# A PSUM bank by name for every tile, and a new order for the loading phase of a fused cross-attention and gated feed-forward kernel

## The chip, the cores and the metric

The kernel runs on one core of a Trainium2 chip. The metric is the device time of one execution in microseconds (us). Several executions are timed and their median is the kernel's time; one more execution is recorded by the hardware profiler, and all rows of a profile come from that one.

## The reference, cut to what matters

```python
B, H, S, Ns, D = 8, 8, 512, 32, 64            # x (B, H, S, D), state (B, H, Ns, D)
a  = softmax(x @ state.T / sqrt(D))           # per batch and head, 512 x 32
xread = a @ state                             # 512 x 64
a2 = softmax(state @ x.T / sqrt(D))           # 32 x 512
sread = a2 @ x                                # 32 x 64
attn = concatenate([xread, sread], axis=2)    # 544 rows for each batch and head
X = attn.transpose(0, 2, 1, 3).reshape(8 * 544, 512)
out = (sigmoid(X @ w_gate) * (X @ w_val)) @ w_out   # w_gate, w_val 512 x 1536, w_out 1536 x 512
```

## The kernel before, in words

All matrix operands are bf16, sums are fp32. For a batch `b` the kernel never forms `xread`. It multiplies the state with the weights first (`sw_visit`, `sw_wide`, `sw_six`: `SW` = state x `w_gate` and state x `w_val`, 128 rows for a group of heads) and then multiplies that with the transposed attention `aT` (`gv_mm`, `gv_half`, L345 and L357): the result is the gate and the value product of 128 hidden features for the 512 rows of the batch. ScalarE takes the tanh of one half (`gv_th`, L366), VectorE makes the gated product from it and the other half (`gv_glu`, L371). The product with `w_out` is done plainly for batch 0 (`out_mm`, L384) and in seven products of half the size, in Strassen's manner, from then on (`w_mm`, L427, with the sums of `t_sum` and `s_sum`). The `sread` rows of all batches are handled together at the end as a ninth batch (L360, L446, L463).

The steps for one batch's attention: `xT_mm` transposes x on TensorE (batches 0 and 1) or `at_xT_dma` does so by DMA (later ones); `S_mm` or, for batch 0 by quarters, `Sq_mm` makes the scores; `S_exp`/`Sq_exp` the exponential on ScalarE; `n_sum`/`nq_sum` and `n_mul`/`nq_mul` the softmax's sums and the scaled `ab`; `aT_mm` with `aT_cp`, or `aT_dma`, the transpose `aT`; `at_Eb` casts the exponentials and `rd_mm` with `rd_fin` makes the `sread` rows.

The schedule is by hand: every engine runs its instructions in the order in which the program issues them. PSUM has eight banks, each of which holds one tile. In the kernel before they belong to four pools: `GV` (two banks), `SWP` (four), `OU` and `AT` (one each); a pool with several banks gives each new tile one of its own, and the matmul that writes it waits for the last reader of the tile that had it.

The program has two parts. The first, a flat list of calls from `pre = wp.tile(...)` to `rd_fin(2)`, loads and casts everything, does all of batches 0 and 1 but the end of batch 1's output product, and prepares batch 2. The loads stand on three queues: SP has `load_xp(0, ...)` (four parts of x(0)), later `load_x(3)`, the DMA transposes and the stores; POOL has `load_xh(1, ...)`, ten weight loads `load_w(w, lo, n)` (w 0 is the gate, 1 the value; `lo` the first hidden column), three `load_sb`, three `load_wo` and `load_x(2)`, mixed with its own casts and products; ScalarE's has `load_s(0)`. `warm(n, bank)` issues n matmuls on a zero tile (L496), which compute nothing that is used. `sw_cp(b, lo, w, e, engine)` copies a bank of `sw_visit(b, lo, n)` to `SW`. The second part is a loop, `step(b, f)` for b from 2 to 8 and f from 0 to 11, with the feature products of batch b, the output products of batch b - 1 and the attention of batch b + 1.

Lines of the profile that are called by several steps: L96 `cast_xp`, L117 `cast_x`, L133/L136 `xT_mm`/`xT_cp`, L175 `Sq_mm`, L187 and L189 `nq_sum`, L194 `nq_mul`, L209 `n_sum`, L235/L245 `aT_mm`/`aT_cp`, L287 and L294 the products of `SW`, L331 `sw_cp`, L519/L530 the transposes and copies of the state, L83, L88, L101, L105 the loads.

Of the kernel before, what the change touches and what calls it, by code (L numbers as in the profile page):

```python
# [16 lines left out]
def kernel(  # L17
# [14 lines left out]
    nc = tc.nc  # L32
# [40 lines left out]
    AT, OU, GV, SWP = (p_at, "at"), (p_out, "outp"), (p_gv, "gv"), (p_sw, "swp")  # L73
# [224 lines left out]
    def sw_visit(b, lo, n, *ws):  # L298

        if b not in SWs:  # L300
            SWs[b] = fp.tile((128, 2, 2, dff), BF, name="SW", bufs=2)
        if not ws:
            pss = [p_sw.tile((128, 512), FP, name="swp", tag="swp") for e in range(2)]
            sw_pair(pss, b, lo, n)
            for e in range(2):
                sw_left[b, lo, 2, e] = (SWs[b][:, e, :, lo:lo + n], pss[e].rearrange("p (w n) -> p w n", w=2))
        for w in ws:
            pss = [p_sw.tile((128, 512), FP, name="swp", tag="swp")[:, :n] for e in range(2)]
            sw_mm(pss, b, w, lo, n, 0)
            for e in range(2):  # L310
                sw_left[b, lo, w, e] = (SWs[b][:, e, w, lo:lo + n], pss[e])

    def sw_wide(b, v, other=AT):
# [4 lines left out]
        for k, places in enumerate(((OU, other), (SWP, SWP), (SWP, SWP))):  # L318
            pss = [p[0].tile((128, 512), FP, name="swp", tag=p[1]) for p in places]
# [17 lines left out]
    def gv_mm(b, f, place):  # L337
# [3 lines left out]
        for w in range(2):  # L341
            ps = place[0].tile((128, 512), FP, name="gvp", tag=place[1])[:, :n]
# [75 lines left out]
    def w_mm(b, k, c):  # L418
# [4 lines left out]
        if first and c == 0:  # L423
            place = OU if key in (1, 5) else SWP
# [15 lines left out]
    def p_mm(k, part):  # L440
        c, lo, n = parts[part]
        lhs, rhs = prod(B - 1, k)
        if k == 7:
            wps["p", part] = p_sw.tile((128, 512), FP, name="outp", tag="swp")[:, :n]
# [10 lines left out]
    def q_mm(k):  # L455
# [3 lines left out]
        if k == key:  # L459
            place = {1: AT, 2: SWP, 5: GV, 7: GV}[k]  # L460
# [80 lines left out]
    pre = wp.tile((128, 2), FP, name="pre")  # L541
    nc.vector.memset(wm, 0.0)
    warm(1, GV)
    load_xp(0, nc.sync, 6, 2)
    nc.gpsimd.memset(xs[:, :, :, D:], 1.0)
    zero(sTd, pool)
    load_s(0, nc.scalar)
    warm(2, OU)
    cast_s(0, act)
    warm(4, SWP)  # L550
    zero(sbz, vec)
    load_xp(0, nc.sync, 4, 2)
    cast_xp(0, act, 6, 2)
    zero(sTz, vec)
    warm(1, AT)
    make_identity(nc, ident)
    sT_mm(0, SWP)
    xT_mm(0, 3, GV)
    cast_xp(0, vec, 4, 2)
    sT_pad(1, act)  # L560
    xT_cp(0, 3, act)
    xT_mm(0, 2, AT)
    sT_pad(0, vec)
    load_xp(0, nc.sync, 2, 2)
    cast_xp(0, vec, 2, 2)
    xT_cp(0, 2, vec)
    warm(1, OU)
    load_xh(1, 0, 4)
    load_xh(1, 4, 4)
    load_w(1, 256, 256)  # L570
    load_xp(0, nc.sync, 0, 2)
    Sq_mm(0, 3, SWP)
    load_w(0, 256, 256)
    Sq_exp(0, 3)
    cast_xp(0, act, 0, 2)
    xT_mm(0, 1, SWP)
    warm(1, SWP)
    Sq_mm(0, 2, AT)
    xT_mm(0, 0, GV)
    xT_cp(0, 1, act)  # L580
    load_w(1, 1024, 256)
    Sq_mm(0, 1, SWP)
    warm(1, GV)
    nq_sum(0, 3)
    nq_mul(0, 3, vec)
    load_w(0, 1024, 256)
    xT_cp(0, 0, vec)
    Sq_exp(0, 2)
    load_sb(2)
    warm(2, SWP)  # L590
    nq_sum(0, 2)
    Sq_mm(0, 0, OU)
    xT_mm(1, 0, SWP, 2)
    warm(1, AT)
    nc.vector.memset(ones, 1.0)
    Sq_exp(0, 1)
    Sq_exp(0, 0)
    xT_cp(1, 0, act, 2)
    warm(2, SWP)
    xT_mm(1, 2, AT, 2)  # L600
    S_mm(1, 0, SWP)
    nq_sum(0, 1)
    load_w(1, 0, 256)
    nq_sum(0, 0)
    load_w(0, 0, 256)
# [96 lines left out]
    cast_x(2, pool, 4, 4)
    sT_cp(1, act)
    sT_mm(3, AT)
    gv_th(1, 9)
    gv_glu(1, 9)
    nc.scalar.activation(pre[:, 0:1], ones, AF.Exp)
    gv_th(0, 4)
    gv_mm(0, 6, GV)
    sw_cp(1, 512, 1, 0, act)  # L710
    sw_visit(1, 512, 512, 0)
    sT_cp(3, act)
    gv_glu(0, 4)
    sw_cp(1, 512, 1, 1, vec)
    cast_x(2, pool, 0, 4)
    gv_th(0, 6)
    gv_glu(0, 6)
    gv_mm(0, 5, SWP)
    at_xT_dma(2)
    load_x(3, nc.sync)  # L720
    sw_cp(1, 512, 0, 1, vec)
    gv_mm(0, 7, GV)
    pad(2, 6)
    gv_th(0, 5)
    sw_cp(1, 512, 0, 0, act)
    gv_glu(0, 5)
    gv_th(0, 7)
    sw_wide(2, 1)
    sw_cp(2, 1, 0, 1, act)
    t_sum(0, nc.gpsimd)  # L730
    t_sum(1, nc.gpsimd)
    gv_glu(0, 7)
    gv_mm(1, 6, GV)
    sw_cp(2, 1, 2, 1, act)
    sw_cp(2, 1, 1, 1, act)
    out_mm(0, 0, AT)
    sw_cp(2, 1, 0, 0, vec)
    sw_visit(1, 0, 256)
    sw_cp(2, 1, 1, 0, act)
    sw_cp(2, 1, 2, 0, vec)  # L740
    sw_visit(1, 1280, 256)
    out_mm(0, 7, OU)
    gv_th(1, 6)
    out_mm(0, 9)
    sw_cp(1, 1280, 2, 0, act)
    sw_cp(1, 1280, 2, 1, vec)
    gv_mm(1, 10, SWP)
    gv_th(1, 10)
    out_mm(0, 2)
    sw_cp(1, 0, 2, 1, vec)  # L750
    sw_cp(1, 0, 2, 0, vec)
    gv_mm(1, 1, SWP)
    gv_th(1, 1)
    gv_glu(1, 10)
    gv_glu(1, 6)
    out_mm(0, 4)
    out_mm(0, 11)
    S_mm(2, 0, SWP)
    gv_mm(1, 4, GV)
    gv_mm(1, 5, SWP)  # L760
    gv_glu(1, 1)
    S_exp(2, 0)
    n_sum(2, 0)
    gv_th(1, 4)
    gv_th(1, 5)
    n_mul(2, 0, pool)
    S_mm(2, 1, AT)
    gv_glu(1, 5)
    S_exp(2, 1)
    n_sum(2, 1)  # L770
    out_mm(0, 1, GV)
    sw_wide(2, 0)
    sw_cp(2, 0, 1, 1, act)
    aT_dma(2, 0)
    n_mul(2, 1, pool)
    sw_cp(2, 0, 0, 0, act)
    at_Eb(2)
    sw_cp(2, 0, 2, 1, act)
    sw_cp(2, 0, 2, 0, vec)
    sw_cp(2, 0, 1, 0, act)  # L780
    out_mm(0, 3)
    aT_dma(2, 1)
    out_mm(0, 5)
    gv_mm(1, 7, SWP)
    gv_th(1, 7)
    gv_glu(1, 4)
    gv_mm(1, 11, GV)
    sw_cp(2, 0, 0, 1, vec)
    gv_th(1, 11)
    cast_x(3, vec, 4, 4)  # L790
    cast_x(3, act, 0, 4)
    gv_mm(1, 0, SWP)
    at_xT_dma(3)
    gv_th(1, 0)
    gv_glu(1, 11)
    out_mm(0, 6, GV)
    out_mm(0, 8)
    out_mm(0, 10)
    rd_mm(2, GV)
    gv_glu(1, 0)  # L800
    gv_glu(1, 7)
    load_x(4, nc.sync)
# [197 lines left out]
```

## Time and profile before

| what | value |
|---|---|
| timed runs | 218.07, 214.39 and 217.12 us, median 217.12 us |
| the profiled execution | 214.21 us, of which the span from its first to its last instruction is 212.4 us |
| granted TensorE clock, mean | 1.000 |
| HBM read, written | 18.35 MB, 8.91 MB |
| executed | 5260 instructions |

Times in rows are in us from the start of the span. PE is TensorE's matmuls, PEld its weight loads (they overlap), DVE is VectorE, ACT ScalarE, POOL GpSimd, SP the sync engine's queue. In a timeline row the first number is the start, the second the length, `x8` the number of instructions merged; a bracket tells the idle time before it and what ended it. A matmul's length includes the time until its result is out, so matmuls that follow one another overlap: the gap from start to start is the cost.

### The profile page before, as it was taken

What the parts mean: (1) busy time and instruction counts of PE and PEld (TensorE: products, weight loads), DVE (VectorE), ACT (ScalarE), POOL (GpSimd) and SP (SyncE); (2) the same over time, 40 slices, a digit from 0 to 9 for tenths busy, and PEclk for the clock granted to TensorE, in tenths of its full rate; (3) what the DMA queues carried; (4) which work ended last, traced back from release to release, by engine and by line L of the source; (5) the groups of instructions that cost most, each with busy time, mean ns of one, the idle gap of its engine ahead of it and who ended that gap; (6) DMA issues with size and microseconds to landing.
All of it is one profiled execution on the core that took longest, in us unless ns stands there. A gap on an engine that the chain in (4) does not pass through costs nothing.

```text
span 212.4 us, 5260 instructions
## 1 busy us (share of the span) xinstructions
PE 206.2 (97%) x2056; PEld 129.7 (61%) x2059; DVE 156.1 (73%) x300; ACT 130.7 (62%) x245; POOL 77.2 (36%) x99
## 2 busy tenths in 40 slices
PE   8899999999999999999999999999999999999992
PEld 2555343444665756665656575756666666788992
DVE  3987987484887788668876887587848966774682
ACT  4878878486768567864786478647874583233210
POOL 8989406889148204900292019401500000000000
PEclk9999999999999999999999999999999999999999
DMA  5999999584699337847712621253110400131025
GB/s 193 205 193 199 197 297 192 119 272 90 99 245 244 64 63 253 200 58 213 235 29 56 173 102 30 53 142 133 25 36 0 197 5 0 67 133 49 1 98 151
DMA packets 41608, 27.14 MB, mean 128 GB/s; under 512 B 23664, under 2 KB 39280, under 8 KB 41584
## 3 DMA queue, kind: packets, MB, share of 16 engines
q1 hardware_dynamic: 31376, 20.00, 35.8%
q0 software_dynamic: 9776, 6.49, 19.4%
q10 hardware_dynamic: 432, 0.33, 0.6%
q8 instruction: 16, 0.26, 0.5%
q14 instruction: 8, 0.07, 0.1%
HBM read 18.35 MB, written 8.91 MB: 128 GB/s over the span
## 4 chain that ended last, share of the span: by engine, by line
PE 94%; ACT 2%; DVE 1%; issue 1%; ACTq 0%
PE gvp L357 30%; PE outp L427 29%; PE gvp L345 10%; PE gvp L360 5%; PE outp L384 5%; PE swp L287 4%; PE warm L496 2%; PE outp L463 2%; PE swp L294 2%; PE Sp L148 1%; PE outp L446 1%; PE rdp L263 1%; ACT SW L331 1%; PE aTp L235 1%; PE xTp L133 0%
## 5 line engine op out<-in xcount | busy, mean ns | idle before, releaser
L371 DVE SCALAR_TENSOR_TENSOR glu<-th,gvp 128x512 bf16<-128x512 f32 (+1 forms) x108 | 70.3, 654 | 41.6 <-PE gvp L357 13.3
L366 ACT ACTIVATE th<-gvp 128x512 f32<-128x512 f32 (+1 forms) x108 | 62.1, 577 | 51.8 <-PE gvp L357 35.0
L357 PE MATMUL gvp<-aT,SW 128*128 128x512 bf16 x288 | 77.6, 379 | 0.2
L331 ACT CAST SW<-swp 128x512 bf16<-128x512 f32 x80 | 45.2, 589 | 7.4 <-PE swp L287 5.3
L427 PEld LDWEIGHTS <-Sm 128*128 128x128 bf16 x324 | 31.7, 98 | 12.6
L357 PEld LDWEIGHTS <-SW 128*128 128x128 bf16 x288 | 26.7, 98 | 17.5 <-issue 3.1
L201 POOL CAST Eb<-E 128x256 bf16<-128x256 f32 x32 | 14.2, 477 | 54.0 <-ACT E L168 54.0
L427 PE MATMUL outp<-tw,Sm 128*128 128x256 bf16 x240 | 31.7, 273 | 0.0
L427 PEld LDWEIGHTS <-glu 128*128 128x128 bf16 x240 | 23.5, 98 | 10.2
L345 PE MATMUL gvp<-aT,SW 128*128 128x512 bf16 x96 | 23.1, 380 | 0.1
L427 PE MATMUL outp<-wo,glu 128*128 128x256 bf16 x168 | 22.9, 273 | 0.0
L228 POOL TENSOR_TENSOR ab<-E,ri 128x512 bf16<-128x512 f32 x14 | 14.7, 1048 | 9.8 <-DVE ri L211 9.6
L409 DVE TENSOR_TENSOR Sm<-glu 128x768 bf16<-128x768 bf16 (+1 forms) x32 | 16.7, 526 | 0.0
L345 PEld LDWEIGHTS <-SW 128*128 128x128 bf16 x96 | 8.5, 98 | 10.8 <-issue 1.4
L117 POOL CAST xb<-xf 128x1024 bf16<-128x1024 f32 x10 | 11.3, 1161 | 9.3 <-DMA xf<-in_x_dram 9.2
L435 DVE SCALAR_TENSOR_TENSOR res<-outp,U 128x512 f32<-128x512 f32 x19 | 13.0, 683 | 0.0
L360 PE MATMUL gvp<-xb,wgv 128*128 128x256 bf16 x96 | 12.6, 273 | 0.0
L331 DVE CAST SW<-swp 128x512 bf16<-128x512 f32 x16 | 10.7, 682 | 1.7 <-PE swp L294 1.7
L384 PE MATMUL outp<-wo,glu 128*128 128x512 bf16 x45 | 11.4, 379 | 0.2
L427 PE MATMUL outp<-wo,Sm 128*128 128x256 bf16 x84 | 11.5, 273 | 0.0
L168 ACT ACTIVATE E<-Sp 128x512 f32<-128x512 f32 x14 | 8.4, 597 | 4.9 <-PE Sp L148 3.8
L209 DVE TENSOR_REDUCE rs<-E 128x16 f32<-128x512 f32 x14 | 9.5, 680 | 2.0 <-ACT E L168 2.0
(101 smaller groups left out, 211.9 us busy)
## 6 DMA issues: line engine op xcount, KB each, us to landing
out_dram<-res SPq DMA_DIRECT2D x12, 512.0 KB, 2.9
xf<-in_x_dram SPq DMA_DIRECT2D x5, 1024.0 KB, 7.4
out_dram<-res SPq DMA_DIRECT2D x7, 256.0 KB, 2.7
wo<-in_moe_w_out_dram POOLq DMA_DIRECT2D x3, 512.0 KB, 13.1
xf<-in_x_dram SPq DMA_DIRECT2D x4, 256.0 KB, 3.9
wgv<-in_moe_w_val_dram POOLq DMA_DIRECT2D x4, 256.0 KB, 7.2
wgv<-in_moe_w_gate_dram POOLq DMA_DIRECT2D x4, 256.0 KB, 8.3
xf<-in_x_dram POOLq DMA_DIRECT2D x1, 1024.0 KB, 11.6
```

The lines of the kernel that those rows point to most:

```text
L201: nc.gpsimd.tensor_copy(Ebs[b][:, c], E1s[b][:, c])
L228: (nc.gpsimd if eng is pool else nc.vector).tensor_tensor(half(b, i, abs_), e1, ri.unsqueeze(len(ri.shape)).to_broadcast(e1.shape), ALU.mult)
L331: cp(*sw_left.pop((b, lo, w, e)))
L345: nc.tensor.matmul(ps, SWs[b][:, g, w, fs], aTs[b][:, :, g], start=(g == 0), stop=(g == 1))
L357: nc.tensor.matmul(ps, SWs[b][:, g, w, fs], aTs[b][:, :, g], start=(g == 0), stop=(g == 1))
L360: nc.tensor.matmul(ps, (wg, wv)[w][:, j, fs], held["XS"][:, j], start=(j == 0), stop=(j == 3))
L366: nc.scalar.activation(th, held["gv", b, f][0], AF.Tanh, scale=0.5)
L371: nc.vector.scalar_tensor_tensor(glus[b][:, f], held["th", b, f], 1.0, held["gv", b, f][1], ALU.add, ALU.mult)
L384: nc.tensor.matmul(ops[b, c], glus[b][:, f, c * 128:(c + 1) * 128], wo[:, f], start=(f == 0), stop=(f == NF - 1))
L409: eng.tensor_tensor(S_(b, t)[:, i], a, c, op)
L427: nc.tensor.matmul(wps[key][:, c], lhs[:, i, c * 128:(c + 1) * 128], rhs[:, i], start=(first and c == 0 and i == 0), stop=(i == NF // 2 - ...
L435: nc.vector.scalar_tensor_tensor(to, wps[key], 0.5, held["w", name], ALU.mult, ALU.add)
```

## The change

Two things. First, the four PSUM pools become eight pools of one bank each, `G0 G1 OU S0 S1 S2 S3 AT`, and each call names the bank of each tile that it makes. In the step loop the names follow fixed rules (`X(b)`, `gb`, the places in `sw_six`, `p_mm` and `q_mm`); the loop's calls and their order stay. Second, the flat list is written anew: the same calls for the same work, but in another order on every engine and for some of them on another engine.

```diff
-    p_gv = ctx.enter_context(tc.tile_pool(name="p_gv", bufs=2, space=PS))
-    p_out = ctx.enter_context(tc.tile_pool(name="p_out", bufs=1, space=PS))
-    p_sw = ctx.enter_context(tc.tile_pool(name="p_sw", bufs=4, space=PS))
-    p_at = ctx.enter_context(tc.tile_pool(name="p_at", bufs=1, space=PS))
+    banks = [ctx.enter_context(tc.tile_pool(name=f"p{i}", bufs=1, space=PS)) for i in range(8)]
...
-    AT, OU, GV, SWP = (p_at, "at"), (p_out, "outp"), (p_gv, "gv"), (p_sw, "swp")
+    G0, G1, OU, S0, S1, S2, S3, AT = ((p, "b") for p in banks)
+
+    X = lambda b: ((S2, S3), (S3, S2))[b % 2]
...
-    def gv_mm(b, f, place):
+    def gv_mm(b, f, *places):
...
-            ps = place[0].tile((128, 512), FP, name="gvp", tag=place[1])[:, :n]
+            ps = places[w][0].tile((128, 512), FP, name="gvp", tag=places[w][1])[:, :n]
...
-            place = OU if key in (1, 5) else SWP
+            place = OU if key in (1, 5) else X(b)[key == 2]
...
-            place = {1: AT, 2: SWP, 5: GV, 7: GV}[k]
+            place = {1: AT, 2: S0, 5: G1, 7: G0}[k]
...
-        for k, places in enumerate((((SWP, GV), (SWP, SWP), (OU, SWP)) if v else ((OU, GV), (SWP, AT), (SWP, SWP)))):
+        x, y = X(b)
+        for k, places in enumerate((((x, G1), (S0, y), (OU, S1)) if v else ((OU, G0), (x, AT), (S0, S1)))):
...
+        gb = (G0, G1) if nb and v else (G1, G0) if nb or f > 2 else (G0, G0) if f == 2 else (G1, G1) if b == B and f == 0 else (G0, G1)
...
-        gv_half(b, f, 0, GV)
+        gv_half(b, f, 0, gb[0])
...
-                gv_half(b, f, 1, GV)
+                gv_half(b, f, 1, gb[1])
```

The new list, cut to what is issued up to the second feature product, and to the end of the list from the loads of x(3) on (the calls between have the same kinds):

```diff
+    load_xp(0, nc.sync, 6, 2)
     nc.vector.memset(wm, 0.0)
+    warm(3, OU)
+    make_identity(nc, ident)
+    zero(sTd, pool)
+    warm(3, G1)
+    zero(sbz, vec)
+    warm(4, AT)
+    load_xh(1, 0, 4)
+    load_s(0, nc.scalar)
+    cast_xp(0, act, 6, 2)
+    cast_s(0, vec)
+    sT_mm(0, G0)
+    sT_pad(1, act)
+    load_xh(1, 4, 4)
+    zero(sTz, vec)
+    load_xp(0, nc.sync, 4, 2)
+    cast_xp(0, vec, 4, 2)
+    xT_mm(0, 3, G1)
+    load_w(1, 256, 256)
+    xT_mm(0, 2, AT)
+    sT_pad(0, act)
+    xT_cp(0, 3, vec)
+    Sq_mm(0, 3, OU)
+    load_xp(0, nc.sync, 2, 2)
+    load_w(0, 256, 256)
+    warm(2, S2)
...
+    xT_mm(1, 0, S2, 2)
+    nq_sum(0, 3)
+    load_w(1, 1024, 256)
+    warm(4, S3)
+    xT_cp(0, 0, act)
+    nq_sum(0, 2)
+    nq_mul(0, 3, vec)
+    xT_mm(1, 2, OU, 2)
+    Sq_mm(0, 0, AT)
+    load_sb(2)
+    Sq_exp(0, 1)
+    nq_sum(0, 1)
+    nq_mul(0, 2, vec)
+    xT_cp(1, 0, act, 2)
+    xT_cp(1, 2, vec, 2)
+    Sq_exp(0, 0)
+    S_mm(1, 0, G1)
+    S_exp(1, 0)
+    nc.vector.memset(ones, 1.0)
+    S_mm(1, 1, S1)
     nc.gpsimd.memset(xs[:, :, :, D:], 1.0)
+    S_exp(1, 1)
+    load_w(0, 0, 256)
+    sw_visit(0, 256, 256, G0, S3)
+    sw_cp(0, 256, 2, 1, act)
+    load_w(1, 0, 256)
     nq_sum(0, 0)
     nq_mul(0, 0, vec)
+    load_w(1, 1280, 256)
+    n_sum(1, 0)
+    sw_cp(0, 256, 2, 0, act)
+    nq_mul(0, 1, pool)
+    aT_mm(0, AT)
     at_Eb(0)
+    load_w(0, 1280, 256)
     aT_cp(0, 0, vec)
+    sw_visit(1, 256, 256, G1, S1)
+    rd_mm(0, S3)
+    nc.scalar.activation(pre[:, 0:1], ones, AF.Exp)
+    sw_cp(1, 256, 2, 1, act)
+    aT_cp(0, 1, vec)
+    load_sb(1)
+    gv_mm(0, 2, G0, AT)
...
+    aT_cp(1, None, vec)
+    gv_glu(0, 9)
...
+    gv_mm(1, 2, AT, G0)
...
+    gv_mm(1, 6, G0, S2)
...
+    sw_visit(1, 1280, 256, AT, G0)
...
     load_x(3, nc.sync)
...
+    load_x(4, nc.sync)
...
+    cast_x(3, act, 0, 4)
     n_sum(2, 1)
+    out_mm(0, 1, S3)
+    out_mm(0, 3)
+    out_mm(0, 6, S1)
+    sw_wide(2, 0, G1, S0, OU, G0, S2, AT)
     sw_cp(2, 0, 0, 0, act)
+    sw_cp(2, 0, 0, 1, act)
+    sw_cp(2, 0, 2, 1, act)
+    n_mul(2, 1, vec)
+    aT_dma(2, 1)
...
+    out_mm(0, 5)
+    gv_mm(1, 7, G1, G0)
```

More of the change, by code (lines that the diff above doesn't have):

```diff
@@ L443, in p_mm @@
         if k == 7:
[L444 removed]
+            place = (S2, S3, S1)[part]
+            wps["p", part] = place[0].tile((128, 512), FP, name="outp", tag=place[1])[:, :n]
         for i in range(NF // 2):
@@ L560 @@
[L560 to L581, printed above, removed]
@@ L719 @@
-    at_xT_dma(2)
-    load_x(3, nc.sync)
[L721 to L729, printed above, removed]
+    gv_mm(0, 7, G1, S2)
+    gv_th(0, 7)
+    gv_glu(0, 7)
+    sw_wide(2, 1, S1, S0, AT, S3, G1, OU)
+    sw_cp(2, 1, 0, 1, vec)
+    sw_cp(2, 1, 2, 0, act)
+    sw_cp(2, 1, 0, 0, act)
+    gv_mm(1, 6, G0, S2)
+    sw_cp(2, 1, 1, 0, vec)
+    out_mm(0, 7, G1)
+    gv_th(1, 6)
@@ L730 @@
+    out_mm(0, 11)
+    out_mm(0, 4)
+    S_mm(2, 0, S0)
+    S_exp(2, 0)
+    n_sum(2, 0)
+    n_mul(2, 0, vec)
+    aT_dma(2, 0)
+    gv_mm(1, 10, G0, S2)
+    S_mm(2, 1, S3)
     t_sum(0, nc.gpsimd)
     t_sum(1, nc.gpsimd)
[L732 to L747, printed above, removed]
-    gv_th(1, 10)
[L749 to L753, printed above, removed]
-    gv_glu(1, 10)
[L755 to L764, printed above, removed]
+    S_exp(2, 1)
+    gv_th(1, 10)
+    gv_glu(1, 10)
@@ L765 @@
+    gv_mm(1, 5, S1, OU)
     gv_th(1, 5)
-    n_mul(2, 0, pool)
-    S_mm(2, 1, AT)
     gv_glu(1, 5)
-    S_exp(2, 1)
+    cast_x(3, act, 0, 4)
     n_sum(2, 1)
[L771 to L775, printed above, removed]
-    sw_cp(2, 0, 0, 0, act)
-    at_Eb(2)
[L778 to L786, printed above, removed]
@@ L803 @@
+    n_mul(2, 1, vec)
+    aT_dma(2, 1)
+    sw_cp(2, 0, 1, 1, vec)
+    sw_cp(2, 0, 2, 0, vec)
+    out_mm(0, 5)
+    gv_mm(1, 7, G1, G0)
+    out_mm(0, 8)
+    gv_mm(1, 11, S0, AT)
+    sw_cp(2, 0, 1, 0, act)
+    gv_th(1, 7)
+    cast_x(3, vec, 4, 4)
+    gv_th(1, 11)
+    gv_glu(1, 7)
+    at_xT_dma(3)
+    gv_glu(1, 11)
+    gv_mm(1, 0, G1, S0)
+    gv_th(1, 0)
+    gv_glu(1, 0)
+    out_mm(0, 10)
+    at_Eb(2)
+    rd_mm(2, S2)
     rd_fin(2)
```

259 lines of the change are left out of this document (108 added, 151 removed).

## The prediction, made before the changed kernel ran

> **What bounds the kernel now.** I read the page first, then the chain of waits in order of time, then three windows cut where the diff's region starts and ends, then the timeline of the loading phase. Busy columns of the windows: PE, PEld, DVE, ACT, POOL, each with its count, then the granted clock, the DMA share and GB/s.
>
> ```profile
> span 212.4 us, 5260 instructions
> PE 206.2 (97%) x2056; PEld 129.7 (61%) x2059; DVE 156.1 (73%) x300; ACT 130.7 (62%) x245; POOL 77.2 (36%) x99
> 0.00:12.39 12.39, 10.48 (x97) 5.66 (x98) 8.66 (x22) 7.93 (x14) 11.69 (x23) 1.00 1.06 198
> 12.39:53.46 41.07, 40.81 (x455) 18.37 (x458) 30.25 (x54) 30.29 (x58) 28.71 (x31) 1.00 1.05 195
> 53.46:212.40 158.94, 154.91 (x1507) 105.64 (x1506) 117.21 (x225) 92.46 (x174) 36.75 (x47) 1.00 0.40 105
> ```
>
> The reader should see that TensorE is the bound nearly from the first packed state-weight product (`sw_visit(0, 256, 256)`, 12.39) on. The clock is full. Busy alone could hide waits, since a matmul's row lasts longer than the gap to the next, so I look at what a run of matmuls takes in the chain:
>
> ```profile
> 0.99 3.60 PE warm L496 x8
> ...
> 21.89 2.71 PE gvp L345 x12
> 40.26 1.73 PE outp L384 x8
> 168.72 1.02 PE gvp L357 x4
> 170.40 0.86 PE gvp L357 x4
> ```
>
> Eight 512-column matmuls take 1.73 from 40.26 on, 0.216 each, and twelve in a row take 2.71, 0.12 more than twelve times that. So between 12.39 and 53.46 there is little but matmuls at their rate, and the diff takes none of them out: the products named by `sw_visit`, `gv_mm`, `out_mm`, `rd_mm`, `sT_mm` and `sw_wide` are the same set in another order, and even the 17 warm-up matmuls stay 17 (1+2+4+1+1+1+1+2+1+2+1 before, 3+3+4+2+1+4 after). What can be won lies in the start of the stream and in the few waits inside it; what can be lost is new waits.
>
> **The step loop (from 53.46).** The diff changes no instruction and no order there, only bank names. `gb` alternates the two banks as the pool of two did, with three steps near the end that put both halves into one bank, so that the second half waits for the tanh of the first. The row at 168.72 is such a place: 1.02 for four matmuls where 0.86 is usual (170.40). The wait of 0.16 is there already. I cost the loop at nothing; the bound above is two more such waits, 0.3; below, none.
>
> **The start of the stream.** It needs the weights, the scores of batch 0 and their transposes.
>
> ```profile
> 0.73 0.15 POOL L545 MEMSET xs<- 128x64 bf16 x1 [0.29 <-POOLq L984]
> L105 POOL DMA_DIRECT2D wgv<-in_moe_w_gate_dram x1: 770/770/770, 4.6 to 4.6; - x1
> DMA to landing us min/median/max: 7.2/7.2/7.2
> ...
> 11.32 0.61 PE L235 MATMUL aTp<-ident,ab 128*128 128x128 bf16 x8
> 12.39 0.62 PE L294 MATMUL swp<-wgv,tw 64*32 64x512 bf16 x16
> 13.59 2.17 PE L345 MATMUL gvp<-aT,SW 128*128 128x512 bf16 x8
> 15.69 0.63 PE L294 MATMUL swp<-wgv,tw 64*32 64x512 bf16 x16
> ```
>
> The landing line is that of the one gate load issued at 4.6, so it is there at 11.8. Ahead of it on POOL's queue stand the same two loads of batch 1 and the value load; only the memset of `xs` (0.15) moves behind them, so the pack can start at about 11.75 instead of 12.39: at most 0.64 earlier. But before, the transposes of `ab` for batch 0 (from 11.32, 0.52 to the next group) were done by then, and the diff puts them behind the pack. Net on TensorE: 0.1. What then decides is the DVE chain to the first `gv_mm(0, 2)`:
>
> ```profile
> 4.52 0.47 PE L519 MATMUL stp<-ident,sb 128*64 128x128 bf16 x8
> 6.44 0.28 PE L175 MATMUL Sp<-tw,xT 128*128 128x64 bf16 x4
> 9.70 0.42 DVE L187 TENSOR_REDUCE rsq<-E 128x8 f32<-128x256 f32 x1
> 10.15 0.20 DVE L189 RECIPROCAL riq<-rsq 128x8 f32<-128x8 f32 x1
> 10.27 0.91 DVE L194 TENSOR_TENSOR ab<-E,riq 128x256 bf16<-128x256 f32 x2
> 11.10 0.68 DVE L136 COPY xT<-xTp 128x1024 bf16<-128x1024 bf16 x1
> 11.87 0.69 DVE L209 TENSOR_REDUCE rs<-E 128x16 f32<-128x512 f32 x1
> 12.76 0.36 DVE L245 COPY aT<-aTp 128x512 bf16<-128x512 bf16 x1
> 13.05 0.98 ACT SW L331 x2
> ...
> L101 POOL DMA_DIRECT2D xf<-in_x_dram x2: 753/845/937, 2.2 to 3.2; - x2
> DMA to landing us min/median/max: 5.6/5.8/6.0
> ```
>
> After, DVE's order is `xT_cp(1, 2)` (0.68), `nq_sum(0, 0)` (0.65: 0.42 and 0.20 for its reciprocal, from 9.70 and 10.15, and a little between), `nq_mul(0, 0)` (0.45), `n_sum(1, 0)` (0.89, from 11.87 to 12.76), two copies of `aT` (0.36 each). `xT_cp(1, 2)` waits for the transposes of the second half of x(1), which lands at 3.2 + 6.0 = 9.2 and whose eight transposes (0.61, as the eight at 11.32) stand behind four warm-ups; these end near 9.5, so I put the copy at 10.3, 0.8 ahead of its old place at 11.10. The sum is 10.3 + 0.68 + 0.65 + 0.45 + 0.89 + 0.72 = 13.7 for the start of `gv_mm(0, 2)`. Its eight matmuls with those of `gv_mm(0, 3)` need 1.73, which ends at 15.43. Before they ended at 15.69, having taken 2.10 because the second bank of the pack was copied out only at 14.03 (13.05 + 0.98). After, the pack is earlier and both copies are done by about 13.4. Term: **-0.26**. Its ends: 10.3 could be 0.5 later (+0.24) or 0.3 earlier (-0.56).
>
> The very front ends where it did. Ten warm-ups instead of eight (3.60 for eight in the chain) put the state's transposes at about 5.0 instead of 4.52; the two pads of `sTd` follow one another on ACT and end near 6.4, and the first scores start at 6.44 as before. POOL's `nq_mul(0, 1)` and the four casts of `Eb` are covered by the pack.
>
> **Waits inside the stream.** Every bank is now freed by one named reader, so I followed each reuse with the durations of the page (a tanh or copy 0.58 to 0.60 on ACT, 0.49 apart when packed; `gv_glu` and copies 0.69 on DVE, 0.6 apart):
>
> ```profile
> L371 DVE SCALAR_TENSOR_TENSOR glu<-th,gvp 128x512 bf16<-128x512 f32 (+1 forms) x108 | 70.3, 654 | 41.6 <-PE gvp L357 13.3
> L366 ACT ACTIVATE th<-gvp 128x512 f32<-128x512 f32 (+1 forms) x108 | 62.1, 577 | 51.8 <-PE gvp L357 35.0
> L331 ACT CAST SW<-swp 128x512 bf16<-128x512 f32 x80 | 45.2, 589 | 7.4 <-PE swp L287 5.3
> ```
>
> Two come out late. `gv_mm(1, 2)` has its second half in G0, which `gv_glu(0, 9)` must free, and that stands on DVE behind two copies, the `sT` copy and the copy of `aT` for batch 1, all of which the same PE order waits for anyway: **+0.15**. `sw_visit(1, 1280, 256, AT, G0)` needs G0 from `gv_th(1, 6)`, behind two 0.5 copies on ACT: **+0.10**. The rest are freed 0.05 to 1 ahead of need. No weight is the bound: the queue of loads is full in both windows (198 and 195 GB/s) and carries the same bytes in nearly the same order. The bounds of the two: 0 and, if DVE lags one copy more, 0.9.
>
> **The moved load and cast.** `load_x(4)` now stands on SP right behind `load_x(3)`; before, it was issued at 58.5 with `load_x(5)` behind it. And `cast_x(3, act, 0, 4)` moves ahead of four copies of `sw_wide(2, 0)` on ACT; before, they came first (45.67), and the cast at 49.47.
>
> ```profile
> L83 SPq DMA_DIRECT2D xf<-in_x_dram x1: 522/522/522, 40.0 to 40.0; - x1
> DMA to landing us min/median/max: 6.2/6.2/6.2
> ...
> L83 SPq DMA_DIRECT2D xf<-in_x_dram x1: 391/391/391, 58.5 to 58.5; - x1
> DMA to landing us min/median/max: 7.4/7.4/7.4
> ...
> L83 SPq DMA_DIRECT2D xf<-in_x_dram x1: 635/635/635, 59.0 to 59.0; - x1
> DMA to landing us min/median/max: 9.8/9.8/9.8
> ...
> 45.67 2.05 ACT L331 CAST SW<-swp 128x512 bf16<-128x512 f32 x4 [0.86 <-PE swp L287]
> 49.47 1.04 ACT L117 CAST xb<-xf 128x1024 bf16<-128x1024 f32 x1
> 52.76 0.42 PE L266 MATMUL rdp<-xb,Eb 128*32 128x64 bf16 x32
> ```
>
> Each load's issue stands above its landing. After, ACT reaches the cast at about 45.2 with nothing else to do and stands there until x(3) is in; behind it wait the copies, first that of G1, and `gv_mm(1, 7, G1, G0)` needs G1. From 52.76 back, five groups of 0.86 put that product at 48.4. So x(3) must land by 48.4 - 1.04 - 0.59 = 46.8. Alone it lands at 40.0 + 6.2 = 46.2: free. With a load behind it, as the first of the pair, 47.4: a wait of 0.6. I take the middle, **+0.30**, between the only two rows there are. [...]
>
> **Sum.** -0.26 + 0.15 + 0.10 + 0.30 = +0.29 on the profiled execution's 214.21 (span 212.4 and 1.8 around it): 214.5. That execution is 2.91 below the median of the three runs, 217.12, which spread from 214.39 to 218.07; in their terms **217.4**. That is no change for a measurement that tells about 2%.
>
> **The rivals.** *The stream starts early and stays whole.* For it: 0.64 to win at 12.39, the 0.37 lost in 13.59 to 15.69 (2.10 against 1.73); against: the 0.52 of transposes to be paid. With no new wait anywhere: -0.64 + 0.52 - 0.37 = -0.49, so 216.6. A gain of 2% (4.3) would need a third of all that lies ahead of 12.39 gone, and the weights land at 11.8.
>
> *ACT stands at x(3).* One mechanism, at 46.8: if x(3) shares the DMA engines evenly with x(4) it lands like the pair's second, 40.0 + 9.8 = 49.8; the cast ends at 50.9, the copy at 51.4, and TensorE waits from 48.4, 3.0 in all, with everything after it moved: +3.0 in place of +0.30, 220.1. It decides from a landing past 47.8 (a wait of 1.0). Against it: the pair's first landed 2.9 ahead of its second (58.5 + 7.4 = 65.9 and 59.0 + 9.8 = 68.8).
>
> *The names do nothing:* no bank was the bound, and the order alone acts; its time is the forecast's without the two bank terms, 217.1, and I count it there.
>
> **How the numbers follow.** Forecast 0.57 (from -0.4 to +1.0 on 217.1, that is 216.7 to 218.1), early stream 0.25, ACT at x(3) 0.15, something else 0.03. The range takes both rivals' main part and the spread of runs, of which the lowest is 2.73 under the median: low 213.7, high 219.4. Faster by over 2% (under 212.8) 0.03; slower by over 2% (over 221.5) 0.04; within 0.93.
>
> **What would show it.** Right: first `sw_visit` pack near 11.8, `gv_mm(0, 2)` near 13.7, the step loop's first pack within 0.6 of 53.46 and the loop after it 159 long; ACT's idle time before the L117 cast released by the x load. Wrong: the loop's first pack before 52.5 or after 54.5, a step loop that is itself shorter or longer by over 0.5, or a granted clock under 1.0 in the first 15 us.

## The result, and the profile after

| | median | runs | profiled execution | its span |
|---|---|---|---|---|
| before | 214.39 us (214.08 to 218.25) | 19 | 214.21 | 212.4 |
| after | 216.42 us (215.83 to 217.83) | 19 | 216.63 | 214.7 |

The ratio is 1.0078, with a 95% interval of 1.0052 to 1.0103: the changed kernel is slower, by 1.7 us of 214.4, which is less than 2% (the medians of all runs, slow ones included, differ by 2.0). The time lies 1.0 under the 217.4 on record, and inside the range. The difference between the kernels is another matter: +0.29 was forecast, and the 217.4 stood on a median of three runs (217.12) that nineteen runs put at 214.39. So the question is where 1.7 us (2.3 between the two profiled spans) came from.

The same three windows as before, cut at the first pack and at the loop's first pack; columns as there.

```profile
0.00:12.37 12.37, 9.55 (x89) 5.23 (x89) 7.78 (x22) 7.57 (x13) 11.11 (x23) 1.00 1.07 196
12.37:55.60 43.23, 41.27 (x472) 18.80 (x480) 36.01 (x60) 29.48 (x56) 26.98 (x28) 1.00 1.09 211
55.60:214.70 159.10, 154.90 (x1506) 105.28 (x1506) 117.25 (x225) 92.47 (x174) 36.34 (x46) 0.99 0.35 98
```

The start is the same to 0.02, the loop 0.16 longer, and the middle 2.16 longer. Of these, 0.46 is work of TensorE (41.27 against 40.81: transposes that now stand behind the first pack). The time in which TensorE is not busy grew from 0.26 to 1.96, and these 1.70 are most of the 2.3; the 1.96 is the sum of the two waits shown next, 0.78 and 1.18. DVE's busy column in that window rose from 30.25 to 36.01.

Two places hold it. First, TensorE's timeline at the early one:

```profile
12.37 0.41 PE L293 MATMUL swp<-wgv,tw 64*32 64x512 bf16 x8 [0.52 <-DMA wgv<-in_moe_w_gate_dram]
...
14.22 1.89 PE L343 MATMUL gvp<-aT,SW 128*128 128x512 bf16 x8
16.03 0.63 PE L293 MATMUL swp<-wgv,tw 64*32 64x512 bf16 x16
17.44 0.61 PE L234 MATMUL aTp<-ident,ab 128*128 128x128 bf16 x8 [0.78 <-POOL Eb L200]
```

DVE, and then POOL, in the same stretch:

```profile
15.31 1.48 DVE L227 TENSOR_TENSOR ab<-E,ri 128x512 bf16<-128x512 f32 x1
16.71 0.68 DVE L369 SCALAR_TENSOR_TENSOR glu<-th,gvp 128x512 bf16<-128x512 f32 x1
```

```profile
15.19 1.04 POOL L227 TENSOR_TENSOR ab<-E,ri 128x512 bf16<-128x512 f32 x1
16.19 0.81 POOL L104 DMA_DIRECT2D wgv<-in_moe_w_val_dram  x1
```

The transposes `aT_mm(1, AT)` need both products of batch 1 and the bank AT, which `gv_glu(0, 2)` frees. The row names POOL's casts as the releaser, but those at 16.99 are `at_Eb(1)`, which the transposes don't read. What ends last is the glu, at 17.39; it stands on DVE behind the product `n_mul(1, 0, vec)`, and that took 1.48 while POOL made the other product.

The late place, in TensorE's timeline, then DVE's, POOL's and ACT's:

```profile
49.14 0.59 PE L343 MATMUL gvp<-aT,SW 128*128 128x512 bf16 x2
50.92 0.59 PE L343 MATMUL gvp<-aT,SW 128*128 128x512 bf16 x2 [1.18 <-DVE SW L329]
...
54.89 0.42 PE L265 MATMUL rdp<-xb,Eb 128*32 128x64 bf16 x32
```

```profile
46.82 0.68 DVE L208 TENSOR_REDUCE rs<-E 128x16 f32<-128x512 f32 x1
47.53 0.25 DVE L210 RECIPROCAL ri<-rs 128x16 f32<-128x16 f32 x1
47.82 2.45 DVE L227 TENSOR_TENSOR ab<-E,ri 128x512 bf16<-128x512 f32 x1
50.19 1.27 DVE L329 CAST SW<-swp 128x512 bf16<-128x512 f32 x2
```

```profile
46.62 3.09 POOL L400 TENSOR_TENSOR tw<-wo 128x1536 bf16<-128x1536 bf16 x1
49.66 1.50 POOL L251 CAST xs<-xf 128x1024 bf16<-128x1024 f32 x1
```

```profile
47.22 1.04 ACT L116 CAST xb<-xf 128x1024 bf16<-128x1024 f32 x1 [1.50 <-DMA xf<-in_x_dram]
48.17 1.55 ACT L329 CAST SW<-swp 128x512 bf16<-128x512 f32 x3
```

`gv_mm(1, 7, G1, G0)` does its first half in time and then waits for G0. The copy that frees G0, `sw_cp(2, 0, 1, 1, vec)`, stands behind the product `n_mul(2, 1, vec)`, which runs beside `t_sum(2)` on POOL and ends 0.56 after it (50.27 against 49.71). In the kernel before, that subtraction started at 48.93, behind both products and the casts on POOL. ACT did stand idle at x(3) for 1.50, but the first half of `gv_mm(1, 7)`, which needs what ACT copies next, was not held up. The read `rd_mm(2)` starts at 54.89 where it was 52.76: 2.13 later. All operations of line 227, min/median/max in ns, say the same in two rows:

```profile
L227 POOL TENSOR_TENSOR ab<-E,ri x11: 1043/1048/1052, 15.2 to 153.7; 128x512 bf16<-128x512 f32 x11
...
L227 DVE TENSOR_TENSOR ab<-E,ri x3: 691/1475/2446, 15.3 to 47.8; 128x512 bf16<-128x512 f32 x3
```

The same instruction, on the same shape, takes DVE 0.69, 1.48 and 2.45, while POOL's eleven lie within 9 ns of each other. The one of 0.69 is `n_mul(2, 0)`. It meets POOL too, but there it is POOL that is late. DVE, then POOL:

```profile
45.01 0.69 DVE L227 TENSOR_TENSOR ab<-E,ri 128x512 bf16<-128x512 f32 x1
```

```profile
44.73 1.92 POOL L200 CAST Eb<-E 128x256 bf16<-128x256 f32 x4
```

The second of the four casts, recorded from 45.07, just behind the product's start, took 0.89; the other three took 0.39 to 0.40. Here the operation that came second is again the one held, and it is POOL's.

### The profile page after: what moved, and what is told of

It is laid out like the page before. It is cut to its first block, busy times and chain, and to the rows that moved or that the text cites. A ratio compares the mean times of both kernels' runs of the same rounds, so it can differ in the third digit from the quotient of the medians.

```text
span 214.7 us, 5258 instructions
## 1 busy us (share of the span) xinstructions
PE 205.7 (96%) x2059; PEld 129.3 (60%) x2059; DVE 161.0 (75%) x306; ACT 129.5 (60%) x242; POOL 74.4 (35%) x96
## 4 chain that ended last, share of the span: by engine, by line
PE 85%; POOL 4%; DVE 4%; DMA 3%; issue 1%; ACT 1%; POOLq 0%; DVEq 0%; ACTq 0%
PE gvp L355 29%; PE outp L425 28%; PE gvp L343 8%; PE gvp L358 5%; PE swp L286 3%; PE outp L382 3%; DMA xf<-in_x_dram 3%; PE outp L462 2%; PE swp L293 2%; POOL wgv L104 1%; DVE ab L227 1%; PE Sp L147 1%; PE outp L445 1%; POOL Eb L200 1%; DVE glu L369 1%
## 5 line engine op out<-in xcount | busy, mean ns | idle before, releaser
L329 ACT CAST SW<-swp 128x512 bf16<-128x512 f32 x82 | 46.2, 591 | 6.5 <-PE swp L286 4.9
L425 PEld LDWEIGHTS <-Sm 128*128 128x128 bf16 x324 | 31.7, 98 | 12.6
L425 PE MATMUL outp<-tw,Sm 128*128 128x256 bf16 x240 | 31.8, 273 | 0.0
L425 PEld LDWEIGHTS <-glu 128*128 128x128 bf16 x240 | 23.5, 98 | 10.2
L425 PE MATMUL outp<-wo,glu 128*128 128x256 bf16 x168 | 22.9, 273 | 0.0
L227 POOL TENSOR_TENSOR ab<-E,ri 128x512 bf16<-128x512 f32 x11 | 11.5, 1048 | 8.4 <-DVE ri L210 8.2
L425 PE MATMUL outp<-wo,Sm 128*128 128x256 bf16 x84 | 11.5, 273 | 0.0
L251 POOL CAST xs<-xf 128x1024 bf16<-128x1024 f32 x10 | 10.6, 1084 | 0.0
```

Of the source, the lines that this page charges most:

```text
L227: (nc.gpsimd if eng is pool else nc.vector).tensor_tensor(half(b, i, abs_), e1, ri.unsqueeze(len(ri.shape)).to_broadcast(e1.shape), ALU.mult)
L329: cp(*sw_left.pop((b, lo, w, e)))
L425: nc.tensor.matmul(wps[key][:, c], lhs[:, i, c * 128:(c + 1) * 128], rhs[:, i], start=(first and c == 0 and i == 0), stop=(i == NF // 2 - ...
```

## The experiments

Theory: DVE and POOL exclude each other here, two of the three products that moved to DVE meet an operation of POOL that is already running and are held till its end (1.48 and 2.45, where the third takes 0.69), and what stands behind them on DVE is late for TensorE. Rivals: the new names of the banks make the waits; the front of the order, by its extra warm-ups; or the cast at x(3). Three expectations call it the port theory: that name is the author's guess at a cause, and the runs show which operations are held, not why.

For the table I use one interval that starts behind the first loads: from the pack that follows the pair of `gv_mm` of batch 0 (16.03 above) to `rd_mm(2)` (54.89). It is 37.07 before and 38.86 after. It still differs between executions by what the late wait takes in each.

### The late meeting

**t_sum(2) held back.** A tiny copy on POOL reads the end of the product first:

```
+    nc.gpsimd.tensor_copy(gate, abs_[2][:, 3, 1, :1])
     t_sum(2, nc.gpsimd)
```

> A one-element copy on POOL that reads the product of `n_mul(2, 1)` stands ahead of `t_sum(2)`, so POOL's subtraction starts only when VectorE's product is done; VectorE's own instructions are unchanged. Port theory (VectorE's product with two SBUF inputs does not run beside a POOL instruction on SBUF, it stands until that one ends): the product at 47.8 takes 0.69 instead of 2.45, the wait of TensorE in `gv_mm(1, 7)` goes from 1.18 to under 0.2, span 214.7 - 1.2 = 213.5, time 215.2 against 216.4. Rival, ACT standing at x(3) or a VectorE that is simply too full there: the product still ends near 50.3 or the wait stays above 0.8, span 214.5 to 214.9.

DVE, then POOL:

```profile
47.97 0.69 DVE L228 TENSOR_TENSOR ab<-E,ri 128x512 bf16<-128x512 f32 x1
48.58 1.28 DVE L330 CAST SW<-swp 128x512 bf16<-128x512 f32 x2
49.78 2.73 DVE L117 CAST xb<-xf 128x1024 bf16<-128x1024 f32 x1
```

```profile
48.73 0.19 POOL L921 COPY gate<-ab 128x1 bf16<-128x1 bf16 x1 [1.92 <-DVE ab L228]
48.87 3.09 POOL L401 TENSOR_TENSOR tw<-wo 128x1536 bf16<-128x1536 bf16 x1
```

The product takes 0.69 and the wait at `gv_mm(1, 7)` is gone; the interval is 37.51 (53.70 - 16.19), 1.35 less. 215.58 us, ratio 1.004 (1.0022 to 1.0058): by the ratios about half of the slowdown came back, though their intervals just overlap. The held one is now `cast_x(3, vec)`: 2.73, where it took 1.31 in the profile after and 0.68 in the kernel before. Nobody waits for it.

**The product back on POOL.**

```
-    n_mul(2, 1, vec)
+    at_Eb(2)
+    n_mul(2, 1, pool)
...
-    at_Eb(2)
```

> One part undone: `n_mul(2, 1)` is back on POOL, behind `at_Eb(2)`. Port theory: no long product is left there, POOL's takes 1.05 at about 47.8, the two copies of `sw_wide(2, 0)` on VectorE are done by 49.1, no wait in `gv_mm(1, 7)`, span 214.7 - 1.3 = 213.4. Rival, ACT standing at x(3): that cast still starts at 47.2, the copies behind it are as late as before, the wait stays near 1.2, span 214.6 to 214.8.

The product took 1.05 on POOL, no wait stood at `gv_mm(1, 7)`, and the interval was 37.52, as with the copy. ACT still stood at x(3), for 1.31, and it cost nothing. 215.92 us, ratio 1.007 (1.0039 to 1.0102); the profile agrees with the run above, while the ratios' intervals overlap and can't tell the two from each other.

**POOL busy, but only writing.**

```
-    t_sum(2, nc.gpsimd)
+    nc.gpsimd.memset(T[:, 2], 0.0)
+    nc.gpsimd.memset(T[:, 2], 0.0)
```

> t_sum(2) on POOL is replaced by two memsets of the same tile (about 1.4 each, by the 0.95 of the memset of 128x1024): POOL is busy as long, but reads nothing. It leaves that subtraction out. Theory (a DVE operation with two inputs in SBUF and a POOL operation that reads SBUF exclude each other): the product n_mul(2, 1) on DVE takes 0.69 as when alone, and the 1.2 wait at gv_mm(1, 7) is gone. Rival (whatever POOL does in SBUF, writes too, or the load of the DMAs in that stretch, slows DVE): 1.5 or more, and the wait stays in part.

DVE, then POOL:

```profile
48.35 0.69 DVE L227 TENSOR_TENSOR ab<-E,ri 128x512 bf16<-128x512 f32 x1
```

```profile
47.88 1.38 POOL L921 MEMSET tw<- 128x1536 bf16 x1
```

The product lies wholly inside the second memset (48.35 to 49.04 in 47.88 to 49.26) and takes 0.69. The interval is 37.52. That POOL is busy is not enough to hold the product: the memsets only write, and beside them it is not held.

**One input in place of two.**

```
-    n_mul(2, 1, vec)
+    nc.vector.tensor_copy(half(2, 1, abs_), half(2, 1, E1s))
```

> In the changed kernel the product n_mul(2, 1) on DVE is replaced by a copy of the same 128x512 elements, which reads one tile of SBUF and not two; t_sum(2) on POOL stays. It leaves the scaling of that half by 1/sum out. Theory (only an operation with two inputs in SBUF is held): the copy takes 0.4 to 0.7 beside POOL's t_sum(2), and the wait at gv_mm(1, 7) is gone. Rival (any DVE operation that reads SBUF is held while POOL reads two tiles): 1.5 or more.

DVE, then POOL:

```profile
48.03 2.30 DVE L776 CAST ab<-E 128x512 bf16<-128x512 f32 x1
```

```profile
46.95 3.10 POOL L400 TENSOR_TENSOR tw<-wo 128x1536 bf16<-128x1536 bf16 x1
```

This part of the theory fell: a copy with a single input is held as well (2.30, till 0.28 after POOL's end), and TensorE waited 0.9. But neither is every reader held: the reduction over the exponentials at 46.82 in the profile after (0.68) reads the same tile beside the same `t_sum(2)`, and takes no longer than the other reductions of that form there (0.674 to 0.686, fourteen of them).

**The meeting put into the kernel before.** Old pools of banks, old order, two edits:

```
-    n_mul(2, 1, pool)
+    n_mul(2, 1, vec)
     sw_cp(2, 0, 0, 0, act)
+    t_sum(2, nc.gpsimd)
     at_Eb(2)
...
-    t_sum(2, nc.gpsimd)
```

> The kernel before, with n_mul(2, 1) on DVE in place of POOL, and t_sum(2) moved on POOL ahead of the casts of Eb, so that the two meet there as they do after the change. No bank and no other order changes. Theory (the meeting alone makes the stall): the product takes 1.5 to 3 us in place of 0.69, the copy and the glu behind it on DVE come 1 to 2 late, TensorE waits for them before rd_mm(2), and the time goes up by 0.8 to 1.8 (ratio 1.004 to 1.009). Rival (the new names of the banks make the stall, since they tie gv_mm(1, 7) to the copy behind the product; with the pools of before another bank would have been free): the product may be held, but rd_mm(2) starts within 0.3 of 52.76 and the ratio is below 1.002.

TensorE, DVE, POOL:

```profile
48.21 0.59 PE L345 MATMUL gvp<-aT,SW 128*128 128x512 bf16 x2
50.36 2.48 PE L345 MATMUL gvp<-aT,SW 128*128 128x512 bf16 x10 [1.55 <-DVE SW L331]
```

```profile
46.65 3.05 DVE L228 TENSOR_TENSOR ab<-E,ri 128x512 bf16<-128x512 f32 x1
49.63 0.68 DVE L331 CAST SW<-swp 128x512 bf16<-128x512 f32 x1
```

```profile
46.06 3.09 POOL L402 TENSOR_TENSOR tw<-wo 128x1536 bf16<-128x1536 bf16 x1
```

216.47 us, ratio 1.0065 (1.0028 to 1.0102). The same wait stands at the same product without any named bank, and the interval is 38.94 in place of 37.07. The names of the banks are not needed for it.

### The early meeting

**The product moved ahead on DVE.**

```
+    n_mul(1, 0, vec)
     n_sum(1, 1)
...
-    n_mul(1, 0, vec)
```

> `n_mul(1, 0)` stays on VectorE but goes ahead of `n_sum(1, 1)`, so that it runs while POOL issues loads and not beside POOL's `n_mul(1, 1)`; no instruction more or less. Port theory: it takes 0.69 instead of 1.48, the bank that `aT_mm(1)` needs is free at about 16.9 instead of 17.4, TensorE's wait there falls from 0.78 to 0.3, span 214.7 - 0.5 = 214.2. Rival, VectorE simply holds too much work ahead of `gv_glu(0, 2)`: the order of the same work changes nothing, the wait stays at 0.7 to 0.8, span 214.6 to 214.8.

DVE, then TensorE:

```profile
14.36 0.68 DVE L227 TENSOR_TENSOR ab<-E,ri 128x512 bf16<-128x512 f32 x1
```

```profile
17.17 0.62 PE L234 MATMUL aTp<-ident,ab 128*128 128x128 bf16 x8 [0.24 <-POOL ab L227]
```

The product takes 0.68 and TensorE's wait falls from 0.78 to 0.24, now for POOL's product, whose sums come later on DVE. 216.23 us, ratio 1.0075 (1.0049 to 1.0101): in the time it can't be seen, since the two ratios' intervals overlap almost wholly.

**Both products of batch 1 on POOL,** as before the change, and the two loads behind them:

```
     load_w(0, 1280, 256)
+    n_mul(1, 0, pool)
     aT_cp(0, 0, vec)
...
-    load_sb(1)
...
     n_sum(1, 1)
+    n_mul(1, 1, pool)
+    load_sb(1)
...
-    n_mul(1, 0, vec)
...
-    n_mul(1, 1, pool)
```

> Only the two products of batch 1 are both put on POOL, one behind the other as before (1.04 each), each as soon as its reciprocals are there. Theory (the product on DVE was held by POOL's, and kept gv_glu(0, 2) from freeing the bank AT): gv_glu(0, 2) ends near 16.0, the transposes of aT for batch 1 start without a wait near 16.7 in place of 17.44, time 0.6 to 0.8 down, ratio near 1.005. Rival (POOL's second product, 16.0 to 16.4, is then what is late, as when the DVE product was only moved ahead): a wait of 0.3 or more for POOL stays there, less than 0.4 is won, ratio 1.006 or above.

TensorE's timeline, then its waits (total, times, longest):

```profile
16.55 0.62 PE L234 MATMUL aTp<-ident,ab 128*128 128x128 bf16 x8
```

```profile
PE gvp L343 <- DVE SW L329: 1.4, 1, 1.4
```

No wait is left at the transposes, where it was 0.78. The late one is 1.36, and the interval is 38.21. 216.24 us, ratio 1.006 (1.0031 to 1.0089), which the time alone can't tell from the 1.0078 of the changed kernel. The late wait was 1.18 in the profile after and about 0.5 in the next two runs, so that 1.36 here doesn't show that the edit moved it.

### The front

**Two warm-ups fewer ahead of the transposes of the second half of x(1).**

```
-    warm(4, S3)
+    warm(2, S3)
```

> Two of the four warm-up matmuls ahead of the transposes of the second half of x(1) are left out; they compute nothing that is used. Chain theory (the first feature product waits for the VectorE chain that starts with the copy of these transposes): the transposes start at 9.65 instead of 10.05, `gv_mm(0, 2)` at about 13.9 instead of 14.2, span 214.7 - 0.3 = 214.4. Rival, the weights' landing at 12.3 sets this stretch: the first pack stays at 12.4 and `gv_mm(0, 2)` at 14.1 to 14.3, span 214.6 to 214.8.

TensorE's timeline, its late wait, and line 227 on DVE:

```profile
12.05 0.41 PE L293 MATMUL swp<-wgv,tw 64*32 64x512 bf16 x8
12.98 0.61 PE L234 MATMUL aTp<-ident,ab 128*128 128x128 bf16 x8 [0.53 <-DVE ab L193]
...
PE gvp L343 <- DVE SW L329: 0.5, 1, 0.5
...
L227 DVE TENSOR_TENSOR ab<-E,ri x3: 737/1475/1689, 15.5 to 48.2; 128x512 bf16<-128x512 f32 x3
```

216.36 us, ratio 1.008 (1.0054 to 1.0106): nothing. The weights came earlier in this execution, and TensorE then waited 0.53 for the last product of batch 0. DVE, busy without a gap there, is what the start of the stream waits for. The last two rows are the late meeting, which this edit leaves alone: here `t_sum(2)` started at 46.20, 1.96 ahead of the product at 48.16, where it was 1.20 ahead in the profile after (46.62 and 47.82). The product was held for 1.69 and not 2.45, and TensorE waited 0.54 and not 1.18.

**Two warm-ups fewer ahead of the state's transposes, one pad on DVE.**

```
-    warm(4, AT)
+    warm(2, AT)
...
-    sT_pad(0, act)
+    sT_pad(0, vec)
```

> Two of the four warm-ups ahead of the state's transposes go, and the second pad of sTd moves from ACT to DVE, which stands idle there (5.3 to 5.9 us). Theory (the ramp is late by what is late at the very front: state transposes at 5.11, first scores at 6.94): transposes near 4.7, first scores near 6.3, the DVE chain and gv_mm(0, 2) 0.3 to 0.5 earlier (about 13.1 to 13.3 in place of 13.59), and about 0.3 of the time back: ratio 1.006. The stall at the transposes of aT for batch 1 and the one at gv_mm(1, 7) stay. Rival (the gate weights, landing between 11.8 and 12.6, bind, or the chain's later links do): gv_mm(0, 2) stays within 0.1 of 13.6 and the ratio within 1.007 to 1.009.

```profile
PE Sp L174 <- DVE xT L135: 1.1, 2, 0.9
...
PE aTp L234 <- DVE ab L193: 0.5, 1, 0.5
```

The transposes came at 4.51, and the first scores still at 6.94: the copy of xT now stood behind the pad on DVE. `gv_mm(0, 2)` started at 14.23 (14.22 after). 216.77 us, ratio 1.0092 (1.0063 to 1.0121). A miss: the edit did not make the front earlier. Since the pad moved too, it doesn't tell what the two warm-ups alone do. The late wait was 0.53 here.

**The kernel before once more.**

> The kernel before once more, for a second look at its front. Theory (the landing of the first loads differs by some tenths from one execution to the next, in this kernel as in the others, so that the 12.39 and 12.37 of the first packs say nothing about the change): the gate weights land between 11.7 and 12.7, and the first gv_mm(0, 2) starts between 13.3 and 14.3, not in the same place as before (13.59). Rival (the front of this kernel is steady, and the change made it late): landing within 0.1 of 11.86 and gv_mm(0, 2) within 0.1 of 13.59.

```profile
13.76 2.18 PE L345 MATMUL gvp<-aT,SW 128*128 128x512 bf16 x8
15.86 0.62 PE L294 MATMUL swp<-wgv,tw 64*32 64x512 bf16 x16
```

The gate weights landed at 12.16 in place of 11.86, the pair started 0.17 later and ended at 15.86 in place of 15.69, and the interval was 37.10. The start differs by tenths between executions. In the changed kernel and its variants, eleven profiled executions, the landing lay between 11.79 (the run with the edited front above) and 12.77 (the last one below), for a load issued at 4.54 in both.

### All of it at once

**Both meetings taken away, and the front edited.** The edits of the first, the seventh and the ninth experiment together.

> No product on DVE beside an operation of POOL: both products of batch 1 on POOL, t_sum(2) held back until the product n_mul(2, 1) is done, and the earlier front. Theory (the two held products and the late front make up the whole of the slowdown): 0.8 + 1.2 + 0.3 of about 2.1 are gone, the loop's first pack is within 0.4 of the 53.46 of before, ratio 0.998 to 1.002. Rival (the time goes elsewhere, in the order of the work and the loop): no more than half comes back, ratio 1.004 or above, and new waits stand where the two stalls were.

215.07 us, ratio 1.0014 (0.9985 to 1.0042), interval 36.69, loop's first pack at 53.82 (53.39 in the same view of the kernel before): 0.43 later, just outside the 0.4 expected, and in the time no difference from before is left.

**The same without the edit of the front.**

> The changed kernel with both products of batch 1 on POOL and t_sum(2) held back until n_mul(2, 1) is done; its front is left as it is. Theory (the two held products are the whole of the slowdown, and the edit of the front did nothing): as with the front edited, the loop's first transposed read rd_mm(2) starts near 52.8 to 53.2 and the ratio is 0.998 to 1.002. Rival (the front edit carried part of what came back): ratio 1.003 or above.

The middle window, between the two first packs:

```profile
12.82:54.34 41.52, 41.22 (x472) 18.80 (x480) 34.72 (x59) 29.43 (x55) 27.86 (x30) 1.00 1.14 217
```

214.72 us against 214.64, ratio 0.9997 (0.9972 to 1.0021). TensorE's time without work in this window is back at 0.30 (before 0.26, after 1.96); the interval is 36.84, 0.23 less than before. `rd_mm(2)` started at 53.63, not at the expected 52.8 to 53.2, as the weights landed latest of all in this execution, at 12.77, and the interval began at 16.79.

The two waits of TensorE, the interval, and what is left of the interval without them:

| | early wait | late wait | interval | without the waits | ratio |
|---|---|---|---|---|---|
| before, two executions | 0 | 0 | 37.07, 37.10 | 37.07, 37.10 | 1 |
| after | 0.78 | 1.18 | 38.86 | 36.90 | 1.0078 |
| after, two edits of the front alone | 0.78, 0.78 | 0.54, 0.53 | 38.22, 38.21 | 36.90, 36.90 | 1.008, 1.0092 |
| product ahead on DVE, early | 0.24 | 0.95 | 38.10 | 36.91 | 1.0075 |
| t_sum held back; product on POOL, late | 0.78, 0.78 | 0, 0 | 37.51, 37.52 | 36.73, 36.74 | 1.004, 1.007 |
| both on POOL, early | 0 | 1.36 | 38.21 | 36.85 | 1.006 |
| neither; the same with the front edited | 0, 0 | 0, 0 | 36.84, 36.69 | 36.84, 36.69 | 0.9997, 1.0014 |
| before, with the late one | 0 | 1.55 | 38.94 | 37.39 | 1.0065 |

Without the two waits the changed kernel and its variants agree to 0.22 (36.69 to 36.91), so the two waits, 1.96 together in the profile after, are more than all that its interval has over the kernel before (1.79). The early one is 0.78 wherever its code is unchanged. The late one has no fixed price: 0.53 to 1.18 with the same code from 16.03 on, and 1.55 in the kernel before. The time shows each as well: the run without any meeting (up to 1.0021) lies below the two with the early alone (from 1.0022 and 1.0039) and the one with the late alone (from 1.0031), below the first of these by very little. No version ran faster than the kernel before.

## Why the prediction was right on the time and wrong in its working

That nothing large would be won or lost was right: the largest single wait is 1.2 of 214. That 216.42 lies so near to 217.4 is luck. The base of 217.12 was 2.7 too high, the cost of the change was put at 0.29 and measured at 1.7, and the two errors go against each other. On the profiled execution the same sum gave 214.5, and 216.63 was measured. The time lies below the forecast's own 216.7 to 218.1 and beside the 216.6 of the rival whose stream starts early, which it did not do (12.37).

Of the prediction's signs, the loop's length and ACT's stand at x(3) came out. The first pack (12.37 for 11.8) and `gv_mm(0, 2)` (14.22 for 13.7) did not, and the loop's first pack at 55.60 is past the 54.5 that it named as a sign of being wrong. Where the loss sits was not foreseen. Step by step:

- *The change part by part: the product moved to DVE.* This is the step that failed. `n_mul(1, 0)`, `n_mul(2, 0)` and `n_mul(2, 1)` moved from POOL to DVE and got no term; in the sum they cost nothing. Measured: 1.48, 0.69 and 2.45, and 0.78 + 1.18 = 1.96 of waiting on the path. The trace of before held a warning that the prediction does not use. DVE, then POOL, in the loop of the kernel before:

```profile
65.38 1.08 DVE L409 TENSOR_TENSOR Sm<-glu,Sm 128x768 bf16<-128x768 bf16 x1
```

```profile
65.00 1.05 POOL L228 TENSOR_TENSOR ab<-E,ri 128x512 bf16<-128x512 f32 x1 [0.64 <-DVE ri L211]
```

  The other operations of that form have a median of 0.55. This one met a product on POOL that was already running (65.00 to 66.05), took 1.08 and ended 0.41 after it. By that row the meeting of `n_mul(2, 1)` with a 3.09 long subtraction could have been priced: its end plus about half a microsecond.
- *The start of the stream, -0.26.* Wrong sign. The pair ended at 16.03, +0.34. `xT_cp(1, 2)` came at 10.71 and not at 10.3, and the last product of batch 0 on DVE took 0.61 and not 0.45, beside POOL's casts. The pack came at 12.37 and not at 11.75, since its weights landed at 12.33. Over executions the pair ended at 15.69, 15.86 and 16.42 in the kernel before and the one with the late meeting, and at 15.99 to 16.79 (median 16.31 of eleven) in the changed one and its variants: later by some 0.4, with a spread as large. Which of the edits of the front makes it, stays open; both attempts on warm-ups left it.
- *The very front, first scores at 6.44 as before.* 6.94 in the profile after, but 6.40 to 7.42 over its variants and 6.28 to 6.61 in the two further executions of the old front. Only partly the change.
- *The bank terms, +0.15 and +0.10.* No wait stood at `gv_mm(1, 2)` or at `sw_visit(1, 1280)`. Both are 0.
- *ACT standing at x(3), +0.30.* ACT stood there as said, and in the profile after the price was 0, since `gv_mm(1, 7)` itself came at 49.14 and not at 48.4. In the run with neither meeting ACT stood 1.99 and TensorE was late by some 0.15: `gv_mm(1, 7)` started at 49.22, when ACT's first copy behind the cast ended (48.59 and 0.58 long), and 1.02 behind the four matmuls ahead of it, which took 0.87 in the profile after. In the profile after, x(3) and x(4) together:

```profile
L82 SPq DMA_DIRECT2D xf<-in_x_dram x2: 448/486/523, 40.9 to 41.6; - x2
...
DMA to landing us min/median/max: 6.3/7.6/8.9
```

  The first needed 6.3 (6.2 alone before, 7.4 as the first of a pair), and landed at 47.2, although the other was issued 0.7 behind it and landed at 50.5. So here the later load did not hold up the earlier one; why the pair of before needed 7.4 is not shown. The 6.3 lies at the lower of the two rows between which the prediction took the middle. The rival that took the pair's second landing, 49.8, falls: ACT stood 1.50 and TensorE waited for none of it.
- *The loop at nothing, 159 long.* 159.10 against 158.94, within its bound of 0.3. One new wait stands in it: six matmuls of L425 need 0.93 to the next group, where the same six needed 0.66 before (151.65 to 152.31).

```profile
153.62 0.82 PE L425 MATMUL outp<-tw,Sm 128*128 128x256 bf16 x6
154.55 0.59 PE L355 MATMUL gvp<-aT,SW 128*128 128x512 bf16 x2
```

  It stands in all ten variants of the changed kernel too (0.90 to 0.93) and in neither other execution of the old order (0.65, 0.66); why it came is not settled.

Without the two meetings the changed order is worth about what the sum said, nothing that can be measured (0.9997).

Side by side, what DVE did while an operation of POOL was already running: a product was held beside a product (1.48) and beside a subtraction (2.45, 3.05) and free beside a memset (0.69), a cast from one input was held beside a subtraction (2.30), a reduction was free beside one (0.68). The theory on record for the one-input run, that only an operation with two inputs is held, fails on the cast. What makes these operations wait for each other is not shown.

## What to carry to other kernels

Before moving an operation between DVE and POOL, lay the two timelines side by side and see which of the two starts first where they meet. If an operation of POOL that reads, as the product and the subtraction here, is already running, price a DVE product or cast of SBUF data by the end of that operation (1.48, 2.45 and 2.30 here), not by its own duration (0.69 for the product), and look at what stands behind it on DVE; if DVE comes first, look behind POOL's (here a cast of 0.89 for 0.39). A row whose maximum is far from its minimum, as 691/1475/2446, is the place to look first. And measure a stretch between two events behind the first loads when the loads' landing differs from one execution to the next by more than the effect.

## What the runs showed of the hardware that was not expected

- A held DVE product ended 0.55 to 0.56 after POOL's operation: 50.27 against 49.71, 16.79 against 16.23, 49.70 against 49.15. The held copy of one input ended 0.28 after it: 50.33 against 50.05. POOL's own operation, which had come first, kept its 1.04 or 3.09 to 3.10 each time. Where DVE came first it was POOL's cast that took longer, 0.89 for 0.39.
- DVE's copies from PSUM that ran beside POOL were not held: the two at 50.19 in the profile after took 1.27 together beside POOL's cast, and the pair at 48.58 in the run with `t_sum(2)` held back took 1.28 beside that subtraction.
- The same load, issued at 4.54 to 4.55 in all eleven executions, landed up to 0.98 apart.
